# Attention, then a SoLU feed-forward: w_in loaded and converted later, v loaded by ScalarE in quads 1 to 4, one row sum moved

## Chip, cores and metric

One core of one Trainium2 chip. The metric is the time of one execution in microseconds (us) on the device; lower is better.

## The reference

Two blocks in a row, all float32 (the w_ weights and the feed-forward gain g arrive as float64):

```python
# q, k, v: (8, 12, 448, 64)
q_n, k_n = rmsnorm(q, g_q), rmsnorm(k, g_k)      # over the 64 of a row
attn = softmax(q_n @ k_n.T / 8) @ v
x = attn.transpose(0, 2, 1, 3).reshape(3584, 768)
h = x @ w_in                                     # (768, 1024)
solu = h * softmax(h)
ln = (solu - mean) / sqrt(var + 1e-6) * g_ln
out = ln @ w_out                                 # (1024, 768)
```

## The kernel before

The work has three stages on one core. The attention takes about the first 330 us, the product with w_in (seven half-size products instead of eight, by sums and differences of blocks) runs to about 582 us, the product with w_out after that. The change lies in the attention.

**Quads.** Two heads make a pair n (0 to 47), two pairs make a quad m (0 to 23), with a = 2m and b = 2m + 1. One turn of `for m in range(NQ)` (L1341) emits one quad. The order of instructions on each engine is the program order of that loop (`tc.manual_schedule()`), with a small list of postponed steps: `later(1, f)` runs f after the next `unit`, a unit being a piece of TensorE work.

**TensorE in a quad.** `scores(n, kc)` (L804) for three chunks of keys of each pair; `scores_last` (L818) for the remaining 64 keys of both pairs; `outputs` and `values(b)` (L846, L859), the products with v; `sums` (L870), which adds up the exponentials with matrices of ones. Scores go to three PSUM buffers of tag "t", each freed by ScalarE's exponential of it (`exponentials`, L800). The sums and the small transpose of `norm_gain` use the same three.

**Normalising ahead.** While quad m is computed, q and k of later quads are prepared: `load(n)` (L627, eight transfers of 56 KB, five buffers), issued some three quads ahead; `squares(n)` (ScalarE, L656) for quad m + 2; `row_sums(n)` (VectorE, L664, `part`) and `fold_sums` (GpSimd, L668, `ss`); one quad later `norms_next`, which is `rsqrt_seed` and `rsqrt_step` (ScalarE and VectorE, the reciprocal root `ny`) and `normalise` (GpSimd, L713, `qkn`); then `qk_transpose` (VectorE, L720) and `gain` (ScalarE, L725). `add(n)` (VectorE, L836, `es`) sums two chunks of exponentials for `sums`. From quad 4 on `norms_next` stands at the head of the quad (`early`), in quads 1 to 3 further back.

**Leaving a quad.** `inverse(m)` (L889) transposes and inverts the row sums (`r`, `rc`), GpSimd copies parts of `rc` across partitions, `divide(m)` (L905), postponed by one unit, writes `xo`, which has one buffer; `store_x(m)` (L914) writes it to DRAM in the next quad.

**Queues.** In the attention every load and store is issued by SyncE's queue in program order: per quad v (`load_v`, one transfer of 384 KB and two of 32 KB, two buffers), the store of xo, two `load`s, and, where one is due, a piece of w_in (512 KB). Only the very first loads of k are issued by ScalarE.

**w_in.** It comes as twelve float64 pieces, `wq[0:12]`. `load_next` loads the next one; `begin(m)` takes a piece in hand in each quad of the list `steps_at` and runs its first part (two ScalarE instructions); `step(m - 1)` runs the second part, the join (two VectorE instructions, L541 and L542), one quad later; after that the next piece is asked for. `joins_at` says in which quads GpSimd makes the block differences of finished pieces (`combine_in`, L565). Two pieces are asked for in quad 0; then one after each join.

**Also touched.** `norm_gain` (L474) transposes the feed-forward gain on TensorE and copies it out on ScalarE.

Of the kernel before, what the change touches and what calls it, by code (L numbers as in the profile page):

```python
# [366 lines left out]
def fast_path(  # L367
# [24 lines left out]
    nc = tc.nc  # L392
# [243 lines left out]
                    src[b, h0 + g // 2].rearrange("(b t) (x d) -> x t b d", t=32, x=2)[g % 2],  # L636
                )

    def load_v(m):


        d = quads[m] = {}
        b, hp = divmod(2 * m, NP)
        src = v[b, 2 * hp : 2 * hp + 4]
        d["v"] = loads.tile([P, 4, NJ, D], FP32, tag="v", name="v", bufs=2)
        d["vl"] = loads.tile([P, 2, D], FP32, tag="vl", name="vl", bufs=2)
        nc.sync.dma_start(
            d["v"].rearrange("p h j d -> p h (j d)"), src[:, 0 : NJ * P].rearrange("h (p j) d -> p h (j d)", j=NJ)
        )
        for i in range(2):  # L650
            nc.sync.dma_start(d["vl"][i * D : (i + 1) * D], src[2 * i : 2 * i + 2, NJ * P : S].rearrange("h p d -> p h d"))
# [68 lines left out]
    def qk_transpose(n):  # L720
        d = st[n]
        d["qkT"] = work.tile([P, 2, S], FP32, tag="qkT", name="qkT", bufs=3)
        nc.vector.transpose(d["qkT"].rearrange("p s t -> p (s t)"), d["qkn"].rearrange("p b d -> p (b d)"))  # L723
# [94 lines left out]
    def scores_last(m):  # L818

        s = ps_t.tile([P, 2, 512], FP32, tag="t", name="s")  # L820
        for i in range(2):
            for h in range(2):
                hh = slice(h * D, (h + 1) * D)
                qkT = st[2 * m + i]["qkT"]
                nc.tensor.matmul(  # L825
                    s[i * D : (i + 1) * D, h, 0:S], qkT[hh, 1, NJ * P : S], qkT[hh, 0, :], start=True, stop=True
                )
        exponentials(quads[m], NJ, s)
# [7 lines left out]
    def add(n):  # L836
        d = st[n]
        d["es"] = work.tile([P, 2, S], FP32, tag="es", name="es")
        nc.vector.tensor_tensor(d["es"], d["E", 0], d["E", 1], OP.add)  # L839
# [19 lines left out]
    def values(n):  # L859


        d = st[n]
        for kc in range(NJ):
            for h in range(2):
                nc.tensor.matmul(  # L865
                    d["o"][h * D : (h + 1) * D, :], quads[n // 2]["v"][:, n % 2 * 2 + h, kc], d["E", kc][:, h],
                    start=False, stop=(kc == NJ - 1),
                )
# [404 lines left out]
    def unit(f, steps=4):  # L1273
        nonlocal now
        f()
        now += steps
        due = [x for x in todo if x[0] <= now]
        todo[:] = [x for x in todo if x[0] > now]
        for _, g in sorted(due, key=lambda x: x[0]):
            g()  # L1280
# [1 line left out]

    wq = [(moe_w_in, c + k, i) for c in range(HD) for k in (0, HD) for i in range(2)]
    n_in = len(wq)
    steps_at = (2, 3, 4, 5, 6, 8, 10, 12, 14, 16, 18, 20)
    joins_at = {7: (0,), 9: (1,), 11: (2,), 13: (3,), 15: (4,), 17: (5,), 19: (6,), 21: (7,), 22: (8, 9), 23: (10, 11)}
    wq += [(moe_w_out, c + k, i) for c in range(HF) for k in (0, HF) for i in range(2)]
    again = [(w, w.shape[0] // P, i) for w in (moe_w_in, moe_w_out) for i in range(-(-w.shape[0] // P * w.shape[1] // S))]
    extent = consts.tile([P, len(again)], FP32, name="extent")
# [6 lines left out]
    def load_next():  # L1296
        if len(raws) < (n_in if conv is None else len(wq)):
            raws.append(load_w(wq[len(raws)]))
# [22 lines left out]
    with tc.manual_schedule():  # L1321
# [19 lines left out]
        for m in range(NQ):  # L1341
            a, b = 2 * m, 2 * m + 1

            def outputs():
                values_last(m)
                values(a)


            next1 = m + 1 < NQ
            next2 = m + 2 < NQ  # L1350
            next3 = m + 3 < NQ
            if m == 0:
                unit(lambda: scores(a, 0))
                normalise_rows(1, 0)
                normalise_rows(1, 1)
                unit(lambda: scores(a, 1))
                unit(lambda: scores(a, 2))
                for s in range(2):
                    transpose_rows(1, s)
                    take_rows(1, s)  # L1360
                squares(2)
                add(a)
                row_sums(2)
                fold_one(2)
                unit(lambda: scores_last(m))
                squares(3)
                rsqrt_seed(norms["one", 2])
                rsqrt_step(norms["one", 2])
                normalise(2)
                unit(lambda: scores(b, 0))  # L1370
                row_sums(3)
                fold_one(3)
                unit(lambda: scores(b, 1))
                unit(lambda: scores(b, 2))
                rsqrt_seed(norms["one", 3])
                rsqrt_step(norms["one", 3])
                normalise(3)
                qk_transpose(2)
                gain(2)
                add(b)  # L1380
                load_v(1)
                load(6)
                load(7)
                for _ in range(2):
                    load_next()
                unit(outputs)
                squares(4)
                qk_transpose(3)
                gain(3)
                unit(lambda: values(b))  # L1390
                squares(5)
                unit(lambda: sums(m))
                inverse(m)
                row_sums(4)
                row_sums(5)
                fold_sums(2)
                later(1, lambda m=m: divide(m))
                continue
            early = 3 < m and next1
            def norms_next():  # L1400
                rsqrt_seed(norms[m + 1])
                rsqrt_step(norms[m + 1])
                normalise(a + 2)
                normalise(b + 2)

            if early:
                norms_next()
            for x in joins_at.get(m, ()):
                combine_in(x)
            if next1:  # L1410
                load_v(m + 1)
            unit(lambda: scores(a, 0))
            store_x(m - 1)
            if early:
                qk_transpose(a + 2)
                if next3:
                    load(a + 6)
            if m == 3:
                norms_next()
            unit(lambda: scores(a, 1))  # L1420
            if m == 2:
                norms_next()
            unit(lambda: scores(a, 2))
            if m == 3:
                qk_transpose(a + 2)
                load(a + 6)
            if m == 1:
                norm_gain()
            unit(lambda: scores_last(m))
            if m < 2:  # L1430
                add(a)
            unit(lambda: scores(b, 0))
            if m == 1:
                norms_next()
                load(a + 6)
                load(b + 6)
            if m == 2:
                qk_transpose(a + 2)
                load(a + 6)
            unit(lambda: scores(b, 1))  # L1440
            if early or 1 < m < 4:
                qk_transpose(b + 2)
                if next3:
                    load(b + 6)
            if m > 1:
                add(a)
            unit(lambda: scores(b, 2))
            if m == 1:
                qk_transpose(a + 2)
            scarce = m < 5  # L1450
            if next2:
                squares(a + 4)
                if not scarce:
                    squares(b + 4)
                row_sums(a + 4)
            if next1:
                gain(a + 2)
            if m == 1:
                add(b)
                qk_transpose(b + 2)  # L1460
            if next1:
                gain(b + 2)
            if scarce:
                squares(b + 4)
                if m > 1:
                    add(b)
            if next2 and m > 1:
                row_sums(b + 4)
                fold_sums(m + 2)
            if not scarce:  # L1470
                add(b)
            add_more(a)
            add_more(b)
            unit(outputs)
            step(m - 2)
            begin(m)
            step(m - 1)
            if m - 1 in sets:
                load_next()
            unit(lambda: values(b))  # L1480
            if m == NQ - 1:
                block_sums(0, 0)
                block_sums(0, 1)
                load_x(1)
            unit(lambda: sums(m))
            inverse(m)
            if m == 1:
                row_sums(b + 4)
                fold_sums(m + 2)
            if next1:  # L1490
                later(1, lambda m=m: divide(m))
            if m == NQ - 2:
                load_x(0)
                sizes(0)
# [191 lines left out]
```

## Time and profile before

| | us |
|---|---|
| median of 3 executions | 824.48 (823.45 to 826.74) |
| the profiled execution | 822.29 |
| its span, first to last instruction | 819.9 |
| TensorE busy in it | 799.1 (97%) |
| VectorE busy | 671.6 (82%) |
| ScalarE busy | 460.8 (56%) |
| GpSimd busy | 462.0 (56%) |

The busy time in 40 equal slices of the span (each digit is tenths, 9 is 90% or more):

```profile
PE   8988999999999999999999999999889999999996
DVE  6868897887878878589999999999996866866945
ACT  6677787776877766255655445442425464464420
POOL 1334556455555557322254378776487867777861
DMA  7777787877777744225554534542458456466312
```

PE is TensorE, DVE VectorE, ACT ScalarE, POOL GpSimd, and SPq the issuing queue of SyncE. The attention is the first sixteen slices, of which the first four (to 82 us) hold quads 0 to 3 and the start of quad 4. A row of a timeline gives start, duration, engine, line, operation, what is written from what, and in brackets how long the engine had been idle and what the profile takes for the releaser.

### The profile page before, as it was taken

Reading aid. Unit: us, or ns where it says so; the run is one execution under the profiler, and the core shown is the slowest. Engines: PE = TensorE matmul, PEld = TensorE weight load, DVE = VectorE, ACT = ScalarE, POOL = GpSimd, SP = SyncE. Lnnn points to the kernel's source line nnn. Section 1 sums busy time; section 2 is a strip of 40 time slices with the busy share of each in tenths; the row PEclk is TensorE's granted clock in tenths of the full one; section 3 lists DMA queues with packets and bytes.
Section 4 is the critical chain, followed back from the end, with each engine's and each line's share of the span. In section 5 each row is a group of like instructions: output and inputs, shape, how many; then the busy total and the mean of one; then the engine's idle time right before and its main releaser. Section 6 shows DMA issues by size and latency. Waiting matters only on the chain.

```text
span 819.9 us, 14946 instructions
## 1 busy us (share of the span) xinstructions
PE 799.1 (97%) x5030; PEld 468.7 (57%) x5030; DVE 671.6 (82%) x1203; ACT 460.8 (56%) x757; POOL 462.0 (56%) x635
## 2 busy tenths in 40 slices
PE   8988999999999999999999999999889999999996
PEld 4333434444444443444444444444589999999996
DVE  6868897887878878589999999999996866866945
ACT  6677787776877766255655445442425464464420
POOL 1334556455555557322254378776487867777861
PEclk9999999999999999999999999999999999999999
DMA  7777787877777744225554534542458456466312
GB/s 134 147 163 183 161 195 148 183 162 156 175 163 177 158 109 123 81 79 165 157 149 141 138 90 121 154 136 69 140 152 269 141 198 234 133 235 209 120 59 82
DMA packets 271938, 122.74 MB, mean 150 GB/s; under 512 B 190444, under 2 KB 257004, under 8 KB 271852
## 3 DMA queue, kind: packets, MB, share of 16 engines
q1 hardware_dynamic: 256668, 111.79, 51.9%
q10 hardware_dynamic: 15184, 9.90, 4.2%
q8 instruction: 42, 0.69, 0.3%
q14 instruction: 44, 0.36, 0.1%
HBM read 84.94 MB, written 36.70 MB: 148 GB/s over the span
## 4 chain that ended last, share of the span: by engine, by line
PE 87%; DVE 5%; POOL 2%; DMA 1%; issue 1%; SPq 1%; ACT 1%; DVEq 0%; POOLq 0%; ACTq 0%
PE b L982 31%; PE A L1177 14%; PE s L812 12%; PE o L865 11%; PE B L1177 7%; PE sm L884 5%; PE C L1177 3%; PE s L825 2%; PE o L854 2%; SPq L634 1%; DMA v<-in_v_dram 1%; DVE es L839 1%; PE pt L766 1%; DVE part L664 1%; DVE qkT L723 1%
## 5 line engine op out<-in xcount | busy, mean ns | idle before, releaser
L982 PE MATMUL b<-w_in,xg 128*128 128x512 f32 x336 | 151.1, 592 | 0.0
L802 ACT ACTIVATE E<-s 128x896 f32<-128x896 f32 x168 | 139.1, 935 | 17.3 <-PE s L812 16.6
L812 PE MATMUL s<-qkT 64*64 64x448 f32 x1152 | 120.7, 546 | 2.4 <-ACT E L802 1.1
L982 PE MATMUL b<-w_in,xsum 128*128 128x512 f32 x252 | 115.0, 592 | 0.0
L865 PE MATMUL o<-E,v 128*64 128x448 f32 x576 | 113.5, 543 | 0.0
L982 PEld LDWEIGHTS b<-w_in,xg 128*128 128x128 f32 x336 | 63.8, 190 | 80.2 <-issue 76.7
L713 POOL TENSOR_TENSOR qkn<-qk,ny 128x896 f32<-128x896 f32 x46 | 77.2, 1698 | 28.1 <-DMA qk<-in_k_dram 12.8
L674 POOL COPY ss<-part 32x56 f32<-32x56 f32 x88 | 41.8, 475 | 87.5 <-DVE part L664 84.7
L1177 PE MATMUL A<-w_out,sums 128*128 128x192 f32 x392 | 80.1, 327 | 4.0 <-ACT u L1189 2.6
L812 PEld LDWEIGHTS s<-qkT 64*64 64x64 f32 x1152 | 48.1, 163 | 61.5 <-ACT E L802 29.9
L982 PEld LDWEIGHTS b<-w_in,xsum 128*128 128x128 f32 x252 | 47.9, 190 | 60.3 <-issue 57.4
L1060 POOL TENSOR_TENSOR he<-he,mhalf 128x1 f32<-128x1 f32 x28 | 17.1, 610 | 114.5 <-DVE he L1059 112.5
L1177 PE MATMUL B<-w_out,sums 128*128 128x192 f32 x392 | 79.9, 326 | 1.2 <-DVE P L1221 1.2
L865 PEld LDWEIGHTS o<-E,v 128*64 128x64 f32 x576 | 39.2, 137 | 72.7 <-issue 67.5
L1066 ACT ACTIVATE u<-u,shift,he 128x1024 f32<-128x1024 f32 x28 | 34.7, 1240 | 76.7 <-POOL shift L1062 74.1
L1177 PEld LDWEIGHTS A<-w_out,sums 128*128 128x128 f32 x392 | 66.1, 190 | 5.3 <-issue 2.9
L1177 PEld LDWEIGHTS B<-w_out,sums 128*128 128x128 f32 x392 | 66.1, 190 | 1.7 <-DVE P L1221 1.5
L723 DVE STREAM_TRANSPOSE qkT<-qkn 128x896 f32<-128x896 f32 x46 | 48.7, 1090 | 6.6 <-POOL qkn L713 6.6
L839 DVE TENSOR_TENSOR es<-E 128x896 f32<-128x896 f32 x48 | 53.2, 1110 | 0.5 <-ACT E L802 0.5
L563 POOL TENSOR_TENSOR w_out<-w_out 128x384 f32<-128x384 f32 x44 | 50.7, 1158 | 1.9
L664 DVE TENSOR_REDUCE part<-sq 128x28 f32<-128x896 f32 x46 | 48.2, 1079 | 2.1 <-ACT sq L656 0.2
L1177 PE MATMUL A<-w_out,s 128*128 128x192 f32 x224 | 45.6, 326 | 0.8 <-ACT u L1189 0.8
(143 smaller groups left out, 1497.0 us busy)
## 6 DMA issues: line engine op xcount, KB each, us to landing
ur<-ud SPq DMA_DIRECT2D x60, 256.0 KB, 4.8
ud<-ub SPq DMA_DIRECT2D x112, 128.0 KB, 2.2
xd<-xo SPq DMA_DIRECT2D x24, 448.0 KB, 3.3
qk<-in_q_dram SPq DMA_DIRECT2D x184, 56.0 KB, 2.2
qk<-in_k_dram SPq DMA_DIRECT2D x184, 56.0 KB, 2.2
v<-in_v_dram SPq DMA_DIRECT2D x24, 384.0 KB, 3.9
out_dram<-P SPq DMA_DIRECT2D x21, 384.0 KB, 3.6
raw<-in_moe_w_in_dram SPq DMA_DIRECT2D x12, 512.0 KB, 4.8
```

Of the source, the lines that this page charges most:

```text
L563: nc.gpsimd.tensor_tensor(o, p, q, OP.subtract)
L664: nc.vector.tensor_reduce(norms[m]["part"][:, i], st[n]["sq"], AX, OP.add)
L674: e.tensor_copy(ss[g * 32 : g * 32 + 32], part[o * 32 : o * 32 + 32])
L713: e.tensor_tensor(d["qkn"], d["qk"].rearrange("p s b d -> p (s b) d"), y.rearrange("p b -> p b ()").to_broadcast([P, 2 * NB, 32]), OP.mult,)
L723: nc.vector.transpose(d["qkT"].rearrange("p s t -> p (s t)"), d["qkn"].rearrange("p b d -> p (b d)"))
L802: nc.scalar.activation(d["E", kc], s[:, :, 0:S], AF.Exp)
L812: nc.tensor.matmul(s[c : c + D, h, 0:S], d["qkT"][hh, 1, keys], d["qkT"][hh, 0, :], start=True, stop=True,)
L839: nc.vector.tensor_tensor(d["es"], d["E", 0], d["E", 1], OP.add)
L865: nc.tensor.matmul(d["o"][h * D : (h + 1) * D, :], quads[n // 2]["v"][:, n % 2 * 2 + h, kc], d["E", kc][:, h], start=False, stop=(kc == NJ ...
L884: nc.tensor.matmul(sm[g : g + 32, :], ones[:, w], e[:, h, t * S // 2 : (t + 1) * S // 2], start=(x == 0), stop=(x == len(terms) - 1),)
L982: nc.tensor.matmul(o, a[:, c], w_in[i][:, c], start=(c == 0), stop=(c == HD - 1))
L1177: nc.tensor.matmul(k[bank], a[:, c].rearrange("p a i -> p (a i)"), w_out[:, area, i, c], start=begin and c == 0, stop=c == KC - 1, skip_gr ...
```

## The change

Five edits, all in the order of the attention's instructions; no operation is added or left out.

1. w_in: the first two pieces are asked for in quad 2 instead of quad 0, and converted from quad 4 instead of 2; pieces come in quads 4 to 10 one after the other (joins in quads 5 to 11), after that in every second quad as before. The block differences follow in quads 9, 11, 13, 14, 15, 17 and so on.
2. `load_v` takes a queue for its large transfer; that of quads 1 to 4 is issued by ScalarE. Its two small transfers (L651) stay on SyncE's queue.
3. In quad 1 the squares of the second pair come before its gain.
4. In quad 1 the row sums of the second pair and the fold come before `outputs`, not after `inverse`.
5. `norm_gain` moves from quad 1 to quad 3, and from before `scores_last` to after it.

```diff
-    def load_v(m):
+    def load_v(m, queue=nc.sync):
...
-        nc.sync.dma_start(
+        queue.dma_start(
             d["v"].rearrange("p h j d -> p h (j d)"), src[:, 0 : NJ * P].rearrange("h (p j) d -> p h (j d)", j=NJ)
         )
         for i in range(2):
...
-    steps_at = (2, 3, 4, 5, 6, 8, 10, 12, 14, 16, 18, 20)
-    joins_at = {7: (0,), 9: (1,), 11: (2,), 13: (3,), 15: (4,), 17: (5,), 19: (6,), 21: (7,), 22: (8, 9), 23: (10, 11)}
+    steps_at = (4, 5, 6, 7, 8, 9, 10, 12, 14, 16, 18, 20)
+    joins_at = {9: (0,), 11: (1,), 13: (2,), 14: (3,), 15: (4,), 17: (5,), 19: (6,), 21: (7,), 22: (8, 9), 23: (10, 11)}
...
                 add(b)
-                load_v(1)
+                load_v(1, nc.scalar)
                 load(6)
                 load(7)
-                for _ in range(2):
-                    load_next()
                 unit(outputs)
...
             if next1:
-                load_v(m + 1)
+                load_v(m + 1, nc.scalar if m < 4 else nc.sync)
             unit(lambda: scores(a, 0))
...
-            if m == 1:
+            unit(lambda: scores_last(m))
+            if m == 3:
                 norm_gain()
-            unit(lambda: scores_last(m))
...
             if m == 1:
                 add(b)
                 qk_transpose(b + 2)
+                squares(b + 4)
             if next1:
                 gain(b + 2)
-            if scarce:
+            if scarce and m > 1:
                 squares(b + 4)
-                if m > 1:
-                    add(b)
-            if next2 and m > 1:
+                add(b)
+            if next2:
                 row_sums(b + 4)
                 fold_sums(m + 2)
...
             if m - 1 in sets:
                 load_next()
+            if m == 2:
+                load_next()
+                load_next()
             unit(lambda: values(b))
...
             inverse(m)
-            if m == 1:
-                row_sums(b + 4)
-                fold_sums(m + 2)
```

## The prediction

> **What bounds the kernel now.** Quads are numbered as the code's m, 0 to 23. I read the table of 20 us windows first.
>
> ```profile
> 20.00:40.00 20.00, 18.61 (x184) 7.55 (x183) 16.79 (x29) 12.29 (x20) 7.67 (x13) 1.00 0.69 139
> 40.00:60.00 20.00, 17.70 (x176) 6.77 (x167) 12.50 (x20) 14.47 (x22) 7.28 (x20) 1.00 0.75 172
> 60.00:80.00 20.00, 17.51 (x164) 6.31 (x166) 16.26 (x29) 14.27 (x20) 9.49 (x13) 1.00 0.76 172
> 80.00:100.00 20.00, 20.00 (x204) 8.54 (x204) 17.40 (x27) 15.34 (x24) 8.89 (x16) 1.00 0.79 172
> ```
>
> The second number after the window's length is PE's busy time. From 80 to 580 us PE never idles; between 20 and 80 it idles 1.39 + 2.30 + 2.49 = 6.2 us. So the change can win at most about 6 us, and only in quads 1 to 4. Next, who waits there, in the list of waits up to 90 us and the timeline of quad 2:
>
> ```profile
> DVE xo L911 <- DMA xd<-xo: 2.5, 1, 2.5
> PEld sm L884 <- DVE es L839: 3.9, 3, 1.6
> ...
> 48.12 0.22 DVE L704 SCALAR_TENSOR_TENSOR ny<-nx,ny 128x56 f32<-128x56 f32 x1
> 48.42 1.70 POOL L713 TENSOR_TENSOR qkn<-qk,ny 128x896 f32<-128x896 f32 x1 [4.63 <-DMA qk<-in_q_dram]
> ```
>
> The bracket blames a load, but POOL starts right after the reciprocal roots (ny) end at 48.34. Quads 1 to 3 are a ring on DVE and POOL: ny, two normalisations on POOL (1.70 each) with their transposes (1.1), two row sums and two adds (about 1.0 each), r, rc, the divisions, the next ny. PE waits for its last add. ny ends at 33.75, 48.34 and 62.98: 14.6 us a turn against PE's 12.9 us a quad.
>
> SyncE's timeline shows why quad 1 is late, ScalarE's who feeds PE there:
>
> ```profile
> 32.65 3.07 SPq L634 DMA_DIRECT2D qk<-in_k_dram  x4
> 35.82 0.90 SPq L510 DMA_DIRECT2D raw<-in_moe_w_in_dram  x2
> 36.81 0.38 SPq L647 DMA_DIRECT2D v<-in_v_dram  x1
> 38.62 0.54 SPq L916 DMA_DIRECT2D xd<-xo  x1
> ...
> 27.08 0.94 ACT L656 ACTIVATE sq<-qk 128x896 f32<-128x896 f32 x1
> 27.92 2.51 ACT L802 ACTIVATE E<-s 128x896 f32<-128x896 f32 x3
> 30.75 1.73 ACT L802 ACTIVATE E<-s 128x896 f32<-128x896 f32 x2 [0.27 <-PE s L825]
> 32.38 0.33 ACT L694 ACTIVATE ny<-ss,eps 128x56 f32<-128x56 f32 x1
> ```
>
> The store of quad 0 was ready at 31.7 but is issued at 38.62, behind v and two w_in blocks of 512 KB; with one xo buffer DVE stops 2.5 us for it.
>
> The last view is the opening, where ScalarE already issues loads beside SyncE:
>
> ```profile
> 1.77 0.51 ACTq L738 DMA_DIRECT2D x<-in_k_dram  x1
> 4.14 0.32 ACTq L738 DMA_DIRECT2D x<-in_k_dram  x1
> DMA to landing us min/median/max: 2.5/2.9/3.3
> L766 PE MATMUL pt<-warm x10: 539/954/1113, 1.4 to 7.6; 128*128 128x448 f32 x10
> 810.00:819.90 9.90, 3.69 (x23) 3.30 (x21) 2.64 (x8) 0.00 (x0) 0.00 (x0) 0.79 0.35 126
> ```
>
> The operands in the trace name a completion semaphore for each transfer: eight of them, dealt in program order over both queues, each transfer waiting until the transfer eight places before it has landed. ScalarE's fourth load, free of any buffer, is issued 1.9 us after its third had gone: it waited for a transfer that SyncE had issued at 1.18 and that landed about 2.9 later. This decides my forecast.
>
> **What the Trainium skill says.** "DMA: Bandwidth & Descriptors", section on the anatomy of one DMA, says that a semaphore wait of a transfer happens on the issuing sequencer; the 4.14 agrees. Its section "Issuing engines are not separate DMA queues" says a second issuer saves only issue time: so the move of v buys SyncE about 0.45 us a quad and no bandwidth. "TensorE: Matmul & The Clock Gate", "What's actually happening", gives half clock after an idle window of about 3.4 us and full clock after a busy one; the warm-up matmuls at 954 ns, the last ones at 539, and the 0.79 of the last window agree. "SBUF — State Buffer", "Who interferes with whom", has a DVE instruction with two SBUF inputs exclude a GpSimd one that reads SBUF: beside the w_in join the four fold copies of quad 3 take 1.81 us, without it in quad 2 1.02.
>
> **The change, part by part.**
>
> *w_in later.* Two SyncE issues (0.9) and 1 MB go from 36 us, so the store of quad 0 leaves as soon as load 7 is out, and lands before its buffer is wanted: DVE's 2.5 us stall goes. What is late next is the ring itself. The joins leave quads 3 and 4 (1.37 of DVE each); in quad 3 that shortens the fold by 0.8, and with it ny on ScalarE and the first exponential of quad 4 (74.46). Before the join in quad 4 nothing stalled after 76.4, so its removal is worth nothing. From quad 5 to 11 w_in costs one 512 KB load a quad. The trace has five such quads in a row: the last load of a quad is issued 7.5 us before its squares in quad 3 (issue 74.49, use 82.00) and 3.8 us before in quad 8 (141.49, 145.33): about 0.7 lost per quad. Seven quads, from a similar start, bring it to about its landing time of 2.2. I take 0.3; bounds 0 and 3.
>
> *Row sums first, squares before the gain.* The second sum (1.0) now precedes r and rc; the fold (1.4) precedes the rc copies on POOL, so the divisions begin 0.6 later, but the exponentials lose their 0.64 wait for the fold. Ring of quad 1: normalisation 1.8, transpose 1.1, sum 1.0, add 1.0, transpose 1.1, sum 1.0, fold and rc copies 2.35, divisions 2.6, ny 0.9 = 12.85, where it was 14.6: −1.75.
>
> *Gain transpose, quad 1 to 3.* Quad 1 loses a PE wait for a PSUM buffer and a 0.17 copy (about −0.45 from first exponential to ny). In quad 3 it costs PE about 0.7, inside the 1.0 that PE waits there for the add anyway: 0.
>
> *v by ScalarE.* Only the large transfer moves, one issue of 0.38 to 0.48; its two small companions stay on SyncE. The first lies in the 1.2 us wait ahead of gain at 26.50: nothing. The second stands at the head of quad 1, ahead of all exponentials, and eight places before it in program order stands the first transfer of load 7. SyncE issues the small pieces at 24.38 (2 x 0.65), then load 6 from 25.7 instead of 26.21, eight issues of 0.52, to 29.9. Load 7 begins at 30.0 and its first transfer lands 2.2 later (median of that line), at 32.2. ScalarE's issue ends at 32.6, where the first exponential starts, not at 27.92: 4.7 us late (4.2 with the shortest landing, 1.8; 6.5 if it takes 4). Behind it are seven exponentials, the ny seed, two squares; behind these PE and the ring. The third (quad 2) waits for load 9, landed by 43.7, while ScalarE sits on the gain until 44.9: nothing. The fourth (quad 3) waits for load 11, landed by 59.1, before PE has scores at 61: nothing.
>
> PE has its three score groups done at 28.54 and all three PSUM buffers full; it idles till 33.5, 5.0 us, longer than the idle window, so I expect half clock until about 38.4 (36.9 to 40.3).
>
> *Sum.* ny of quad 1: the seed comes five exponentials (4.0) after 32.6, at 36.6, and ny ends at 38.0 against 33.75 if PE is warm. Ny of quad 2 would be 38.0 + 12.85 = 50.8, +2.5. At half clock PE's fourth and fifth score groups take 1.5 and 1.7 from 33.5, so the seed comes 0.9 later and ny ends at 38.9; the ring gives 38.9 + 12.85 = 51.75, and PE, whose sums then end at 46.65, makes it 51.85: +3.5 (+4.4 if the half clock lasts to 40.3). Quads 2 and 3 turn as before, +3.5; the shorter fold −0.8; w_in later +0.3: +3.0. The span would be 819.9 + 3.0 = 822.9, its execution 822.29 + 3.0 = 825.3. The median shown lies 2.2 above that execution, so 824.48 + 3.0 = **827.5 us**, slower by 0.36%.
>
> **Rivals.**
> 1. *ScalarE is not held* (a free semaphore, or load 7 landed in time), faster. It pays 0.4 us of issue beside a square: ny of quad 1 −0.2, then −1.75 and −0.8: −2.7, or 821.8. For it: SyncE is relieved early. Against: load 7 cannot be issued before 29.9, since load 6 needs its eight issues. It decides if the wait is below about 2.5 us.
> 2. *Held, PE stays at full clock*: +2.5 − 0.8 + 0.3 = +2.0: 826.5. For: the end of PE's gap depends on one landing. Against: a gap of 5.0 fills a whole window or most of two.
> 3. *Held, and w_in without pauses makes SyncE's queue the bound in quads 9 to 13*, slower for certain: squares wait for loads, about 0.7 a quad once the lead of quad 8 is used up, 3 us in four quads more than the forecast: 830.5. For: the shrinking lead above, DMA at 0.80. Against: alternate quads win some back, and DVE had 0.9 to spare in quads with a join. It decides from the quad in which a load is issued less than 2.2 us ahead of its squares.
>
> **How the numbers follow.** Forecast 0.50, rival 1 0.15, rival 2 0.16, rival 3 0.19. A measurement tells about 0.5% here, 4.1 us: faster is below 820.4, slower above 828.6. Slower holds two fifths of the forecast (the longer landing, the longer half clock: 0.20), most of rival 3 (0.17) and a little of rival 2 (0.02): 0.39. Faster needs more than rival 1's own sum, half of it: 0.08. Within: 0.53. Range 822.0 to 831.0: the forecast, rival 2, rival 3's middle and the edge of rival 1; the likeliest case alone has 826.0 to 829.5.
>
> **What would show it.** ScalarE idle from about 28 to 32.5 at the v issue of quad 1, released by the first landing of load 7; PE's first long gap at 28.5 with matmuls of doubled length after it; no wait of xo for xd; ny of quad 2 near 51.8; fold in quad 3 at 1.0. The forecast is wrong if the first exponential of quad 1 starts before 30, if squares wait for qk between quads 9 and 13, or if PE idles after 80 us.

## The result and the profile after

The changed kernel takes 828.40 us (median of 9 executions, 825.39 to 831.45), the kernel before, beside it, 823.45 (9 executions, 822.22 to 826.74): a ratio of 1.0058, with an interval of 1.0037 to 1.0078. The forecast was 827.5, a rise of 3.0. The profiled execution took 827.79 with a span of 825.8; before it was 822.29 and 819.9, so +5.5 and +5.9.

To see where the 5.9 lie, follow one instruction that occurs once a quad: `inverse`'s transpose (L895). Its start in the two traces:

| r (L895) of quad | before | after | later by |
|---|---|---|---|
| 1 | 40.51 | 45.55 | 5.04 |
| 4 | 86.36 | 89.00 | 2.64 |
| 11 | 176.64 | 179.48 | 2.84 |
| 13 | 202.43 | 206.46 | 4.03 |
| 16 | 241.12 | 246.32 | 5.20 |
| 23 | 330.02 | 335.21 | 5.19 |

So 2.64 come from the opening quads, 2.56 from the stretch from quad 4 to quad 16 (2.36 of them after quad 11), and 0.7 from after the attention. The same shows in the table of windows of the changed kernel (length, then busy time of PE, its weight loads, DVE, ACT, POOL; the granted TensorE clock, where 1.00 is full; DMA share, GB/s):

```profile
20.00:40.00 20.00, 14.47 (x130) 5.44 (x126) 12.37 (x25) 10.78 (x17) 5.13 (x12) 0.91 0.58 110
40.00:60.00 20.00, 18.90 (x192) 7.57 (x191) 14.88 (x21) 11.93 (x17) 7.50 (x13) 1.00 0.68 152
60.00:80.00 20.00, 18.00 (x173) 6.99 (x177) 13.88 (x27) 12.92 (x20) 9.23 (x22) 1.00 0.77 165
...
200.00:240.00 40.00, 38.72 (x382) 15.31 (x380) 32.23 (x52) 27.75 (x40) 22.32 (x35) 1.00 0.76 159
```

PE lost 4.1 us in the first window (18.61 before), and it now idles from 200 to 240 us, where it was full (40.00 of 40.00). Between 40 and 80 it gained 1.7: no division waits for the store of xo any more, and the list of waits has no line of xo for xd.

The opening in three timelines of the changed kernel: SyncE's queue, ScalarE (ACTq is its issuing queue), TensorE.

```profile
20.76 6.67 SPq L634 DMA_DIRECT2D qk<-in_q_dram  x4
27.47 2.04 SPq L634 DMA_DIRECT2D qk<-in_k_dram  x4
29.56 1.25 SPq L651 DMA_DIRECT2D vl<-in_v_dram  x2
```

```profile
23.43 0.67 ACT L727 ACTIVATE qkT<-qkT,gcol 128x448 f32<-128x448 f32 x1 [1.72 <-DVE qkT L723]
23.43 0.39 ACTq L647 DMA_DIRECT2D v<-in_v_dram  x1
...
31.44 0.95 ACT L656 ACTIVATE sq<-qk 128x896 f32<-128x896 f32 x1 [4.62 <-DMA vl<-in_v_dram]
31.46 0.44 ACTq L647 DMA_DIRECT2D v<-in_v_dram  x1
32.29 2.51 ACT L802 ACTIVATE E<-s 128x896 f32<-128x896 f32 x3
```

```profile
25.67 2.52 PE L812 MATMUL s<-qkT 64*64 64x448 f32 x24
33.24 1.77 PE L825 MATMUL s<-qkT 64*64 64x448 f32 x8 [5.06 <-ACT E L802]
34.79 3.20 PE L812 MATMUL s<-qkT 64*64 64x448 f32 x24
```

Read them from the end. PE has a gap of 5.06 us and then runs its next eight matmuls in 1.77 us, as forecast. The first exponential of quad 1 starts at 32.29 (forecast 32.6). But ScalarE isn't held at the v of the head of quad 1: that one, at 31.46, goes out at once. ScalarE stands at the squares of pair 5, 4.62 us, and those wait for load 5. (The bracket names vl; what squares read is qk. The last transfer of load 5 was issued at 29.04 and landed at 31.33, while vl landed at 31.68, after the squares had begun: releasers are inferred, and here a neighbour is named.) Load 5 is late because SyncE needs 6.67 us for four issues that took 1.88 in the kernel before:

```profile
20.37 1.88 SPq L634 DMA_DIRECT2D qk<-in_q_dram  x4
```

What it stood for is told by the chain of work that ended last, the view that follows each step of the changed kernel back to what released it:

```profile
23.43 3.15 DMA v<-in_v_dram
26.58 0.02 issue
26.59 0.31 SPq L634
```

SyncE's third transfer of load 5 goes 0.01 us after the **first** ScalarE v has landed. The operands name the completion semaphore of each transfer, which tells why (issue, transfer, queue, semaphore, landing; the list is put together from the operands and the landing events):

```
20.76  qk<-q  SyncE    101  22.66
21.12  qk<-q  SyncE    103  23.31
23.43  v      ScalarE  104  26.58
26.59  qk<-q  SyncE    104  28.47
26.95  qk<-q  SyncE    105  29.13
```

The v and the third transfer of load 5 share semaphore 104, and the v holds the earlier turn. SyncE stands from 21.59 to 26.59: until 23.43 ScalarE has not even issued the v, and it takes 3.15 us more to land. In program order that v stands after all of load 5. Counting eight places back from SyncE's third transfer of load 5, it was dealt among the transfers of load 4, thirteen ahead of its place in the program.

Quads 11 to 16 of the changed kernel, two of ScalarE's squares that wait, and one of TensorE's waits behind them:

```profile
187.97 0.95 ACT L656 ACTIVATE sq<-qk 128x896 f32<-128x896 f32 x1 [0.94 <-DMA qk<-in_k_dram]
...
202.12 0.95 ACT L656 ACTIVATE sq<-qk 128x896 f32<-128x896 f32 x1 [2.20 <-DMA qk<-in_k_dram]
```

```profile
208.80 0.98 PE L825 MATMUL s<-qkT 64*64 64x448 f32 x8 [0.53 <-ACT E L802]
```

Loads come too late for their squares, the exponentials and additions behind these come late, and PE waits for them. The two squares stand in quads 12 and 13.

### The profile page after: what moved, and what is told of

It is laid out like the page before. It is cut to its first block, busy times and chain, and to the rows that moved or that the text cites. A ratio compares the mean times of both kernels' runs of the same rounds, so it can differ in the third digit from the quotient of the medians.

```text
span 825.8 us, 14938 instructions
## 1 busy us (share of the span) xinstructions
PE 800.4 (97%) x5030; PEld 467.8 (57%) x5030; DVE 673.9 (82%) x1203; ACT 461.7 (56%) x757; POOL 462.1 (56%) x635
## 4 chain that ended last, share of the span: by engine, by line
PE 83%; DVE 5%; POOL 3%; SPq 3%; DMA 3%; issue 2%; ACT 1%; DVEq 0%; POOLq 0%; ACTq 0%
PE b L982 31%; PE A L1177 14%; PE o L865 10%; PE s L812 10%; PE B L1177 7%; PE sm L884 4%; PE C L1177 3%; SPq L634 3%; PE s L825 2%; PE o L854 2%; DMA v<-in_v_dram 1%; DVE part L664 1%; POOL ss L674 1%; DMA qk<-in_k_dram 1%; ACT E L802 1%
## 5 line engine op out<-in xcount | busy, mean ns | idle before, releaser
L802 ACT ACTIVATE E<-s 128x896 f32<-128x896 f32 x168 | 139.2, 933 | 16.9 <-PE s L812 16.3
L656 ACT ACTIVATE sq<-qk 128x896 f32<-128x896 f32 x46 | 43.3, 986 | 10.0 <-DMA vl<-in_v_dram 4.6
```

Source lines behind the costliest of these rows:

```text
L656: nc.scalar.activation(d["sq"], d["qk"].rearrange("p s b d -> p (s b) d"), AF.Square)
L802: nc.scalar.activation(d["E", kc], s[:, :, 0:S], AF.Exp)
```

## Experiments

Each is given as its difference from one of the two kernels. In the expectations, theory A is what the chain above says: the first v by ScalarE has an early turn of a semaphore, and SyncE's load 5 waits for it. C is the forecast's own account, that ScalarE is held by the second v. B is the rival to A that the expectation words itself.

| run | median (n) | ratio to before, interval |
|---|---|---|
| e1: after, all v on SyncE | 823.16 (22) | 0.9998, 0.9984 to 1.0013 |
| e2: after, v of quad 1 on SyncE | 822.87 (22) | 0.9990, 0.9979 to 1.0001 |
| e3: before, v of quads 1 to 4 by ScalarE | 827.61 (6) | 1.0058, 1.0040 to 1.0076 |
| e4: after, w_in spaced | 825.34 (21) | 1.0032, 1.0023 to 1.0040 |
| e5: after, all v on SyncE, w_in spaced | 819.96 (6) | 0.9966, 0.9953 to 0.9979 |
| e6: before, w_in later alone | 821.88 (10) | 0.9987, 0.9970 to 1.0004 |
| e7: after, v of quad 1 written late | 827.16 (6) | 1.0057, 1.0036 to 1.0078 |
| e8: before, w_in later and spaced | 819.51 (22) | 0.9974, 0.9960 to 0.9988 |
| e9: after, large v of quad 1 written late | 822.70 (14) | 0.9993, 0.9977 to 1.0010 |
| e10: before, edits 3 and 4 alone | 822.75 (22) | 1.0003, 0.9997 to 1.0010 |
| e11: as e8, one execution, profiled | 818.56 (1) | |

The kernel before ran at 823.0 beside e1 to e4 and at 822.5 to 822.6 beside the others.

**e1 and e2: the queue of v put back, all or one.** Against after, e1 has both lines, e2 only the first:

```diff
-                load_v(1, nc.scalar)
+                load_v(1)
...
-                load_v(m + 1, nc.scalar if m < 4 else nc.sync)
+                load_v(m + 1)
```

> The change, with all v loads back on SyncE's queue. Theory A (the first v on ScalarE's queue is given a completion semaphore ahead of half of load 5, so SyncE cannot issue the rest of load 5 until that v has landed; w_in without pauses costs about 2.6 us later): the hold of 5 us at 21.6 us goes, the first exponential of quad 1 starts near 27.9, ny of quad 2 ends near 46.5, quads 1 to 4 gain 2.6 us on the kernel before, quads 12 to 19 lose 2.6: about 823.5 us, the same as before. Theory B (the loss comes from w_in without pauses alone): still about 828. Theory C (of the prediction: the second v holds ScalarE at the head of quad 1): also about 823.5.

> The change, with only the v of quad 1 back on SyncE; those of quads 2 to 4 stay with ScalarE. Theory A: as with all v on SyncE, within 0.5 us: about 823.5 us, first exponential of quad 1 before 28.5. Theory C: the v of quad 2 still holds ScalarE, first exponential near 32, about 828 us.

Both are back at the time of the kernel before. In e1 that is a sum of two things: r of quad 4 comes at 83.53, 2.83 before that of the kernel before, and r of quad 23 at 330.08, 0.06 after it, so what the opening gains is lost later. e2 decides between A and C, since the v that C blames is still ScalarE's in it. Its ScalarE timeline:

```profile
26.46 0.42 ACTq L647 DMA_DIRECT2D v<-in_v_dram  x1
26.55 0.93 ACT L656 ACTIVATE sq<-qk 128x896 f32<-128x896 f32 x1
27.39 4.12 ACT L802 ACTIVATE E<-s 128x896 f32<-128x896 f32 x5
```

The second v leaves at 26.46 with no wait, and the first exponential follows at 27.39. C falls. The whole cost of edit 2 is one transfer, v of quad 1: 828.4 to 822.9, 5.5 us between the medians.

**e3: v by ScalarE alone.** Against before:

```diff
-                load_v(1)
+                load_v(1, nc.scalar)
...
-                load_v(m + 1)
+                load_v(m + 1, nc.scalar if m < 4 else nc.sync)
```

> The kernel before, with the v of quads 1 to 4 issued by ScalarE and nothing else changed. Theory A: load 5 is held as in the change, the first exponential of quad 1 starts near 32.3 and nothing wins it back: about 5 us more than before, 828.5. Theory B: no difference from before, 823.5.

The hold comes alone as well. SyncE's queue and ScalarE in e3:

```profile
20.26 7.24 SPq L634 DMA_DIRECT2D qk<-in_q_dram  x4
```

```profile
31.38 0.95 ACT L656 ACTIVATE sq<-qk 128x896 f32<-128x896 f32 x1 [4.49 <-DMA qk<-in_k_dram]
...
32.24 2.51 ACT L802 ACTIVATE E<-s 128x896 f32<-128x896 f32 x3
```

Here the bracket names qk itself. None of the other edits is needed for the 5 us gap (4.94 in this trace), and A stands. Alone, the edit costs 4.6 us of the median (823.0 to 827.61).

**e7 and e9: v of quad 1 still by ScalarE, but written later.** e7 moves the whole `load_v(1, nc.scalar)` behind the squares of pair 5; e9 moves only its large transfer there and leaves the two small ones (vl) in place:

```diff
-                load_v(1, nc.scalar)
+                v_big = load_v(1, nc.scalar, late=True)
                 load(6)
                 load(7)
...
                 squares(5)
+                v_big()
```

> The changed kernel, with v of quad 1 still issued by ScalarE but written after the gain of pair 2 and loads 6 and 7 and the squares of pair 4, not ahead of load 6. If what costs is the place of that transfer in the order of the eight semaphores (a late v ahead of the last transfers of load 5), SyncE is not held: first exponential of quad 1 near 27.5, PE without the 5 us gap, and the time of the version with v of quad 1 back on SyncE, 823. Rival, an issue on ScalarE is what costs, wherever it stands: first exponential at 32 and 828.

> As the run before with v of quad 1 issued late by ScalarE, but its two small companions (vl) stay ahead of load 6 on SyncE, as in the changed kernel; only the large transfer is written after the squares of pair 5. If the place of that transfer among the eight semaphores is what costs (theory A): squares of pair 5 start near 26.7, the first exponential of quad 1 near 27.5, PE has no gap of 5 us, because vl is there in time, and the time is that of the version with v of quad 1 back on SyncE, 823. SyncE may be held by that transfer some 1.6 us in load 7 instead of load 5, which nobody waits for. Rival: a large transfer issued by ScalarE beside the loads costs wherever it stands, 827 to 828.

The time of e7 is the one that the rival names, but its trace agrees with neither. Its first exponential starts at 27.64, as A says; but then TensorE stands. SyncE's queue and TensorE in e7:

```profile
34.93 2.60 SPq L651 DMA_DIRECT2D vl<-in_v_dram  x4
```

```profile
37.16 2.45 PE L854 MATMUL o<-E,vl 64*64 64x448 f32 x8 [5.13 <-DMA vl<-in_v_dram]
39.54 6.32 PE L865 MATMUL o<-E,v 128*64 128x448 f32 x24
```

The two small transfers had moved along, behind loads 6 and 7 on SyncE, which itself stood 1.6 us before load 7 until the v had landed (at 30.49), and `outputs` waited 5.13 us for them, again with slow matmuls after it (6.32 for x24, against 4.73 in e9). So e7 made another wait, and its time tells nothing between A and its rival. In e9 that wait is gone. Its ScalarE and its TensorE (line numbers are up to 4 higher here):

```profile
27.10 0.43 ACTq L648 DMA_DIRECT2D v<-in_v_dram  x1
27.36 0.93 ACT L660 ACTIVATE sq<-qk 128x896 f32<-128x896 f32 x1
27.57 0.52 ACTq L648 DMA_DIRECT2D v<-in_v_dram  x1
28.20 4.12 ACT L806 ACTIVATE E<-s 128x896 f32<-128x896 f32 x5
```

```profile
33.27 4.73 PE L869 MATMUL o<-E,v 128*64 128x448 f32 x24
```

No gap, and 822.70. (All of this trace is some 0.6 later than the others from quad 0 on.) The same transfer on the same queue costs nothing from another place. Its semaphore, 105, still has its turn eight places before the first transfer of load 7, which leaves at 31.00, after the v's landing at 30.91; SyncE stood there 1.7 us. The squares of pair 7 then waited 1.05 us for load 7, but TensorE went on without a gap until 43.98.

**e4 and e5: w_in with pauses.** Against after; e5 has e1's lines too:

```diff
-    steps_at = (4, 5, 6, 7, 8, 9, 10, 12, 14, 16, 18, 20)
+    steps_at = (4, 5, 7, 8, 10, 11, 13, 14, 16, 17, 19, 20)
```

(`joins_at` follows.)

> The change, with the conversion of w_in spread out: quads 4, 5, 7, 8, 10, 11, 13, 14, 16, 17, 19, 20, two at a time with a pause, and the block differences moved to fit. Theory A: the idle of PE between 200 and 240 us (1.3 us) and the lag of quads 12 to 19 go, 2.6 us less than the change: about 825.8. Theory B: all of the loss goes, about 823.5. If the lag has another cause than the w_in loads, 828.4 stays.

> The changed kernel with all v on SyncE and the w_in blocks spaced (quads 4, 5, 7, 8, 10, 11 and every second or third after). If w_in without pauses costs about 2.6 to 3 us wherever quad 1 stands, as the spaced version with the held quad 1 showed (825.3 against 828.4), then this one gains it on top of the version with all v on SyncE: 823.2 - 2.7 = 820.5, ratio 0.997; r of quad 16 about 2.8 us before that of the kernel before, and PE without idle time from 80 us on. Rival: the loss of quads 12 to 16 came only because quad 1 had been late; then nothing is gained by spacing here and it takes 823, as the version with all v on SyncE.

Spacing takes 3.1 us off after (828.40 to 825.34) and 3.2 off e1 (823.16 to 819.96). So in the medians the pieces without pauses cost about 3 us, whether quad 1 is late or not; e5's rival falls. Spacing moves the conversions of the pieces along with their loads, and no run parts the two; that it is the loads is read from the waits for qk. The window of e4 over the rest of the attention is full, where after had 248.72 of PE:

```profile
80.00:330.00 250.00, 250.00 (x2460) 104.84 (x2458) 212.63 (x330) 192.06 (x276) 140.75 (x219) 1.00 0.72 162
```

**e6, e8, e11 and e10: one part of the change alone, on the kernel before.** e6 is edit 1 alone; e8 and e11 are edit 1 with the spaced list of e4; e10 is edits 3 and 4 alone. Its expectation names the gain transpose as well, but in its kernel `norm_gain` stands where it stood before, so edit 5 was not tried alone.

> The kernel before with the first edit alone: w_in asked for from quad 2 on without pauses, its joins later. If the prediction's terms hold: the 2.5 us wait of xo for xd goes, the fold of quad 3 is 0.8 shorter, so r of quad 4 comes some 3 us earlier; w_in without pauses takes 2.6 to 3 back by quad 16: 823, no difference. Rival, the row sums are what shortens the ring of quad 1, and the wait of xo only covered other waits: r of quad 4 hardly earlier, and the loads without pauses make it slower, 825.5.

> The kernel before with w_in asked for from quad 2 on and spaced, rows and v as they were. If the gain of the change came from the store that leaves earlier and from the joins leaving quads 3 and 4, it takes 820.5 to 821. If the row sums' order is needed as well (ring of quad 1), less: 822 to 823, and the spaced version with all edits but v is then ahead by that.

> The kernel before with the third and fourth edit alone (gain transpose in quad 3, row sums and squares of quad 1 earlier). The prediction booked 1.75 us of gain in the ring of quad 1 to these. If it is right and the row sums' order is what gains, ny of quad 2 comes 1.75 us earlier: 821.5. Rival, from the spaced versions with and without these edits (ny of quad 4 at 72.96 and 71.62): the gain was the wait of xo for xd alone, and the edits cost 0.7 to 1.3 us, since the fold now stands ahead of the copies of rc; under the wait of xo, which is still there, that is hidden: ring of quad 1 at 14.6 as before, 823.

> The kernel before with w_in later and spaced, once more, for a profile of an execution near its median of 819.5. Expected there: r of quad 4 at 82.7 (3.7 us before that of the kernel before), PE without idle time from 80 to 330 us, and r of quad 23 still more than 3 us early; if instead squares wait for loads in quads 12 to 22 as in the profile of 825.5, spacing doesn't cure it and the difference between executions has another cause.

e6 opens as the forecast's terms say, with r of quad 4 at 82.88, 3.48 before that of the kernel before; by quad 23 its profiled execution is 1.11 behind (331.13), and its median is 0.6 better than before. Spacing takes 2.4 us off it: e8, edit 1 alone and spaced, has the lowest median of all versions, 819.51. e5, with edits 3 to 5 besides, isn't faster, and e10 is no different in time from before (here the rival is right, the forecast's booking wrong). The divisions of quad 1 in e10 still wait, as the list of waits has it:

```profile
DVE xo L911 <- DMA xd<-xo: 2.6, 1, 2.6
```

So the ring was shortened by the store that leaves earlier, not by the row sums. From the end of ny of quad 1 to that of quad 2 it takes 14.59 before, 12.16 in e6 and 13.00 in e1, which is e6 with edits 3 to 5. In e10 it takes 15.55, where the rival has 14.6; of the 0.96 that this is longer than before, an earlier ny of quad 1 makes up 0.50. In e3, whose list of waits has 0.2 us for xd in place of 2.5, it takes 12.34 with none of the edits 1 and 3 to 5. What edits 3 to 5 do to the divisions is seen on GpSimd and VectorE, first in e6:

```profile
41.18 0.88 POOL L903 COPY rc<-rc 32x14 f32<-32x14 f32 x4 [4.25 <-DVE rc L896]
42.13 1.02 POOL L674 COPY ss<-part 32x56 f32<-32x56 f32 x4
```

```profile
40.98 1.09 DVE L664 TENSOR_REDUCE part<-sq 128x28 f32<-128x896 f32 x1
42.10 0.65 DVE L910 STREAM_TRANSPOSE r<-rc 128x448 f32<-128x448 f32 x1
```

and in e1:

```profile
40.34 1.02 POOL L674 COPY ss<-part 32x56 f32<-32x56 f32 x4 [3.63 <-DVE part L664]
41.44 0.30 POOL L675 TENSOR_TENSOR ss<-ss,part 128x56 f32<-128x56 f32 x1
41.81 0.88 POOL L903 COPY rc<-rc 32x14 f32<-32x14 f32 x4
```

```profile
42.73 0.65 DVE L910 STREAM_TRANSPOSE r<-rc 128x448 f32<-128x448 f32 x1 [1.83 <-POOL rc L903]
```

In e6 VectorE does the row sum in the time in which GpSimd copies rc, and divides at 42.10 without a wait. In e1 the sum is done early, and VectorE stands 1.83 us for the copies, which are now behind the fold. In this ring the order of the kernel before was the better one, by 0.8 us.

The groups of ScalarE's squares from 80 to 335 us show what spacing does for the loads; e6, then e11 (busy time and mean ns; then idle time before them and its releasers):

```profile
L656 ACT ACTIVATE sq<-qk 128x896 f32<-128x896 f32 x34 | 32.2, 987 | 9.3 <-DMA qk<-in_k_dram 9.0 <-issue 0.2
```

```profile
L656 ACT ACTIVATE sq<-qk 128x896 f32<-128x896 f32 x34 | 31.5, 1000 | 0.6 <-issue 0.6
```

In e11 r of quad 4 is at 82.92 (3.44 before that of the kernel before), r of quad 23 at 326.57 (3.45): what edit 1 gains in quads 1 to 4 is kept to the end of the attention.

One thing stays open. e8's own profile fell on an execution of 825.51, and there the same group waited 16.3 us for qk, with the same list; twelve of its 22 executions took 818.3 to 819.7, ten 821.8 to 825.5. Without pauses, three of the ten executions of e6 came below 819.7, and its shortest, 818.32, is as short as that of e8 (818.27). So between these two kernels spacing leaves the shortest time as it is and makes it more frequent; the two profiles of e8 and e11 suggest that what sets an execution apart is whether its loads come in time. Nor do late loads need edit 1: in e3, with w_in as in the kernel before, the squares waited 6.1 us for qk after 80 us, in an execution of 829.36. What makes the loads later in some executions wasn't tried.

## Why the forecast was right in the time, and where it was wrong

**The step that failed: which transfer holds which queue.** The record has the transfers "dealt in program order over both queues". From that it follows in the record that of the first v "the first lies in the 1.2 us wait ahead of gain at 26.50: nothing", and that the second holds ScalarE until load 7's first transfer lands. Both are wrong. It is the first v that costs, and it costs on the other queue: it took its turn thirteen transfers early, and SyncE stood 5.0 us (21.6 to 26.6) until it landed. e2 shows that the second is free (issued at 26.46), e3 that the first is enough, e9 that another place makes it free. The trace of before couldn't test the assumption in the attention, since there SyncE alone issues; the opening with two queues agreed with "eight places back", and the record stretched that to the order in which they are dealt.

**Why the sum held for all that.** Both holds end at the same instructions: squares of pair 5 and the exponentials of quad 1 stand one behind the other on ScalarE. Late by the wrong transfer, the first exponential came at 32.29 for 32.6 forecast, PE's gap was 5.06 for 5.0, ny of quad 1 ended at 38.75 for 38.9, ny of quad 2 at 51.72 for 51.85, and quad 4 was 2.64 late for 2.7 (3.5 − 0.8). That the wrong transfer gave the right delay is luck. What follows from a delay of that size, the gap of PE and the later ny, was worked out soundly from rows that were there.

**The half clock: right, and over sooner.** The record cites the Trainium skill, "TensorE: Matmul & The Clock Gate", "What's actually happening", for half clock after an idle window of about 3.4 us. After the 5.06 us gap the eight matmuls take 1.77 us, and in the kernel before 0.98:

```profile
29.68 0.98 PE L825 MATMUL s<-qkT 64*64 64x448 f32 x8 [0.58 <-ACT E L802]
```

The granted clock is 0.91 in the window of 20 to 40 us, and in shorter windows 0.51 from 32.90 to 36.35 and 1.00 from 36.40 to 40.00. So rival 2 (full clock) is out, but full clock was back at about 36.4, before the forecast's 38.4 and before its earliest, 36.9.

**The term that was too small: w_in without pauses, +0.3.** Measured: +2.56 by quad 16 in the traces, 3.1 and 3.2 in the medians of e4 and e5. The lead of the last load of a quad over its squares falls from 5.8 us at pair 13 and 6.1 at pair 17 to 2.3 at pair 29, which is 0.45 or 0.64 a quad by where one starts, for 0.7 in the record. The fall isn't even, and it wasn't in the kernel before: from pair 13 to pair 23 its leads are 7.5, 6.4, 6.6, 6.0, 5.6 and 3.8. What was wrong is "from a similar start": pair 13 had 7.5 us in the kernel before and has 5.8 in the changed one. So the lead was used up at pair 29; its squares waited 0.94 us and those of pair 31 another 2.20. That is rival 3, near its price (3 us above the forecast; 2.3 to 2.9 measured) and in its place, since the two waits lie in quads 12 and 13; the quads are late from 13 to 16. Two of the signs by which the forecast named itself wrong came true: squares wait for qk between quads 9 and 13 (3.1 us), and PE idles after 80 us (1.3 us).

**The ring of quad 1, −1.75: the size right, the owner wrong.** The record booked it to the row sums. Measured 12.97 against its 12.85; but edit 1 alone makes it 12.16 (−2.43, the wait of xo for xd of 2.5), and edits 3 to 5 put 0.8 back. The 0.6 by which "the divisions begin" later was in the record, but was set against a wait of 0.64 elsewhere and left out of the ring's sum, though the divisions stand in it.

**The fold, and the wait of xo: right.** Without the join the four copies of quad 3 take 1.02 us (1.81 before), and no xo waits for xd.

**What wasn't in the sum.** 0.7 us after 335 us: one more wait of PE for GpSimd's sums, 0.59 us at 611.02. It is in six of the eight traces with edits 3 and 4 (not in e5 and e7) and in none of the five without them; what links it to an edit 250 us earlier isn't shown.

So the rise of 5.5 in the profiled execution is 2.6 (forecast) + 2.6 (forecast 0.3) + 0.7 (not forecast), less 0.4 outside of the span. The medians differ by 4.95, where 3.0 was forecast. That 827.5 lies only 0.9 below the 828.40 is in part luck: the 824.48 from which it was counted is 1.03 above the 823.45 that the kernel before takes here.

## What to carry to other kernels

Before a transfer is given to a second queue, look up which completion semaphore it gets and who has the next turn of it: the queue that is relieved can end up waiting for the transfer that was taken from it, and 384 KB that land in 3.15 us then stop every small load behind. When loads are moved into a stretch, follow the lead of each load over its user quad by quad, from the start that the changed kernel has, and ask what happens in the quads after the lead is gone. Try each edit alone, and run it often enough to see the spread: here the first of five, spaced out, is worth 3 us in the median, the second costs about 5 (4.6 alone, 5.5 within the change), and the other three together gain nothing.

## What was not expected of the hardware and its program

- The eight completion semaphores are shared by both issuing queues, and their turns did not follow the program: v of quad 1 was dealt thirteen transfers early (SyncE held 5.0 us in after, 5.6 in e3), and in e9, written much later, it still had its turn before load 7 (held 1.7 us). By which rule they are dealt isn't shown.
- A gap of about 5 us on TensorE costs more than itself: in e7 the 24 matmuls of `values` after a gap of 5.13 took 6.32 us, without it 4.73 (e9).
- Loads that land a little late spread over executions: the same kernel (e8, e11) ran in 818.56 with 0.6 us of idle time ahead of its squares from 80 us on, and in 825.51 with 16.9.
